# The last four microseconds of a decode kernel: output row in column groups of 228 and 284, the wide part's sums ahead of the direct rows, projection in pieces of 16, 8, 5, 2 and 1 rows

## The chip, the cores and the metric

The kernel runs on one core of one Trainium2 chip. The time is device microseconds of that core, the median of several executions. "Span" is the length of one profiled execution; it is 1.4 to 2.0 us shorter than the time of the same run. Engines: PE does matmuls, DVE and ACT copy and compute, SP issues most of the DMA transfers, POOL hands on semaphores.

## The reference, cut to what matters

```
q = x @ wq                                   # 32 heads of 128
p = softmax(q . k_cache / sqrt(128))         # 16384 keys per head
a = (p . v_cache) @ wo                       # wo: 4096 x 512
b = gated MLP of the same x, @ w_out         # 896 x 512
out = g * a + (1 - g) * b                    # one row of 512, bf16; g = sigmoid(sum(x * gate_w))
```

There is one query row. The two caches are 128 MiB each, and everything else is small beside them. The argument of this document lies entirely in the last product, `@ wo`.

## The kernel before: the parts that matter

The 4096 x 512 matrix `wo` is held as 32 blocks ("rows" below) of 128 partitions x 512 columns. It is loaded in pieces, so that PE can begin before the last byte has come:

```
WO_CUTS = (0, 16, 24, 28, 31, 32)     # pieces of 16, 8, 4, 3 and 1 rows
WIDE = 24                             # rows 0..23 are the "wide part"
NC = 2; DQ = D // NC                  # two column groups of 256
```

The wide part puts four rows side by side into four column groups of the PE array, 512 columns each, so its result `d_ps` is four partial output rows on partitions 0, 32, 64 and 96. ACT copies it to SBUF, and a matmul with a vector of ones then adds up the partitions. The last eight rows (the "direct rows") are added straight into the output row `a_ps`, which is split into two halves on partitions 0 and 32:

```
w_ok = act.op(lambda e: e.copy(out=d_sb[:, :], in_=d_ps), wait=[wide part done])   # line 711
def add(lhsT, rhs, wait, ...):                                                     # line 716
    for s in range(NC):
        matmul(a_ps[32*s : 32*s+1, 0:DQ], lhsT, rhs[:, s*DQ:(s+1)*DQ], accumulate)
for j, (a, b) in pieces:
    for k in range(max(a, WIDE), b):
        add(o2[:, k:k+1], wo[:, k*D:(k+1)*D], wait for piece j)
    if b == 28:
        add(ones_f[:, 0:1], d_sb, [w_ok])            # the wide sums, fp32
# DVE copies half 0 to res, ACT copies half 1 (line 731); SP waits for both,
# then stores the 1024 bytes of res
```
(The fence is shortened: waits and lambdas are written in words, and the loop over the two copies is left out.)

The softmax here doesn't subtract the row's maximum and nothing guards it: scores larger than these inputs give would overflow.

## Time and profile before

The median before the prediction was 652.03 us of three runs; with the runs taken later for comparison it was 651.67 us of six (651.55 to 652.07).

The page of the kernel before, its lines on transfers and on the chain that ended last (the digits are tenths of busy time in 40 slices of the span):

```profile
DMA  9999989999999999999999989999999999999898
...
HBM read 279.58 MB, written 0.00 MB: 430 GB/s over the span
## 4 chain that ended last, share of the span: by engine, by line
DMA 4%; PE 0%; SPq 0%; issue 0%; DVE 0%; ACT 0%; ACTq 0%
```

The kernel is bound by its loads: the DMA engines are busy from end to end. The Trainium skill ("DMA: Bandwidth & Descriptors", Specifications) gives 435 GB/s as the ceiling of the fabric; 430 GB/s over the whole span agrees. (Single slices of 16 us on the page show up to 472 GB/s, so only the whole span is compared.) A change after the last load can move only the tail.

The tail in the timeline of the kernel before (columns: start in us, duration in us, engine, line, operation, output<-input, count; in brackets the idle time just before and what ended it):

```profile
646.45 0.59 ACT L711 COPY d_sb<-ps_all 128x512 f32<-128x512 f32 x1 [6.02 <-PE ps_all L106]
646.92 0.31 PEld L716 LDWEIGHTS ps_all<-bufs,o 128*1 128x1 bf16 x8 [1.02 <-DMA bufs<-in_A_wo_dram]
646.92 0.60 PE L716 MATMUL ps_all<-bufs,o 128*1 128x256 bf16 x8 [0.31 <-DMA bufs<-in_A_wo_dram]
647.25 0.20 PEld L716 LDWEIGHTS ps_all<-d_sb,const-float32-1.0 128*1 128x1 f32 x4
647.36 0.60 PE L716 MATMUL ps_all<-d_sb,const-float32-1.0 128*1 128x256 f32 x4
647.91 0.37 PEld L716 LDWEIGHTS ps_all<-bufs,o 128*1 128x1 bf16 x8 [0.47 <-DMA bufs<-in_A_wo_dram]
647.91 0.60 PE L716 MATMUL ps_all<-bufs,o 128*1 128x256 bf16 x8
648.58 0.36 ACT L731 CAST res<-ps_all 1x256 bf16<-1x256 f32 x1 [1.54 <-PE ps_all L716]
648.58 0.41 DVE L731 CAST res<-ps_all 1x256 bf16<-1x256 f32 x1 [6.09 <-PE ps_all L716]
649.03 0.32 SPq L735 DMA_DIRECT2D out_dram<-res  x1
```

PE does the four rows of the third piece as they land, then the wide sums, which are ready by then, waits for the three rows, and does them and the last row. The pause before 647.91 is a wait for a transfer, not for PE.

### The profile page before, as it was taken

The numbers are of one execution on the slowest core, as the hardware profiler recorded it, in microseconds if no ns is written. First come the engines' busy times: TensorE is split into PE (matmuls) and PEld (weight loads), VectorE is DVE, ScalarE is ACT, GpSimd is POOL, SyncE is SP. The second block draws the span as 40 slices with busy tenths as digits, with TensorE's granted clock in tenths as the row PEclk, the third lists the DMA queues.
The fourth block names the chain that finished last, engine by engine and source line by source line (L and its number), as shares of the span: only waits on it lengthen the run. The fifth ranks groups of instructions, "written<-read, shape, count | busy, mean of one in ns | idle before, by whom it ended". The sixth has DMA issues, their size and how long they took to land. (4 is left out here: it accounts for less than half of the span.)

```text
span 650.2 us, 7735 instructions
## 1 busy us (share of the span) xinstructions
PE 423.0 (65%) x2464; PEld 44.4 (7%) x1304; DVE 336.0 (52%) x159; ACT 45.8 (7%) x112; POOL 2.1 (0%) x10
## 2 busy tenths in 40 slices
PE   0547587847387574747857476584747757478767
PEld 0000000000101000010000101000010100001012
DVE  3457848256380845618265370835629075465600
ACT  2200100000001000010100001000010100001011
POOL 1000000000000000000000000000000000000000
PEclk9959788969779696987969798686978968798999
DMA  9999989999999999999999989999999999999898
GB/s 385 462 419 452 452 387 452 452 439 399 452 452 399 439 452 448 391 452 452 407 431 452 452 387 452 452 423 415 452 452 391 448 452 448 391 431 472 390 432 341
DMA packets 6203, 279.60 MB, mean 430 GB/s; under 512 B 695, under 2 KB 826, under 8 KB 1210
## 3 DMA queue, kind: packets, MB, share of 16 engines
q1 hardware_dynamic: 6194, 279.58, 99.6%
q8 instruction: 1, 0.02, 0.0%
q10 hardware_dynamic: 8, 0.00, 0.0%
HBM read 279.58 MB, written 0.00 MB: 430 GB/s over the span
## 5 line engine op out<-in xcount | busy, mean ns | idle before, releaser
L579 DVE TENSOR_TENSOR bufs<-bufs,qb x64 | 281.5, 4419 | 170.8 <-DVEq L86 170.8
L91 PE MATMUL ps_all<-bufs,ident 128*128 x960 | 261.6, 427 | 0.0
L496 PE MATMUL ps_all<-bufs,ident 128*128 x64 | 28.4, 444 | 153.8 <-PEq L86 153.8
L106 PE MATMUL ps_all<-bufs,p_t 128*8 x1024 | 79.2, 385 | 30.7 <-PEq L86 20.1
L564 DVE TENSOR_REDUCE s_sb<-ps_all 128x64 f32<-128x512 f32 x64 | 44.1, 688 | 95.0 <-DVEq L86 95.0
L91 PE MATMUL ps_all<-zero,ident 128*8 128x512 bf16 (+1 forms) x165 | 58.0, 383 | 0.0
L592 ACT ACTIVATE p_t<-s_sb 64x256 f32 (+1 forms) x32 | 13.3, 414 | 433.4 <-ACTq L86 433.0
L496 PEld LDWEIGHTS ps_all<-bufs,ident 128*128 128x128 bf16 x64 | 6.3, 99 | 367.7 <-issue 367.7
L106 PEld LDWEIGHTS ps_all<-bufs,p_t 128*8 x1024 | 17.9, 82 | 163.7 <-issue 163.5
L531 PE MATMUL ps_all<-pick,d_sb 128*128 128x2 f32 x128 | 16.9, 254 | 16.5 <-PEq L86 16.5
L531 PEld LDWEIGHTS ps_all<-pick,d_sb 128*128 128x128 f32 x128 | 15.7, 192 | 34.7 <-issue 34.7
L601 ACT COPY d_sb<-ps_all 128x512 f32<-128x512 f32 x16 | 9.4, 586 | 104.5 <-ACTq L86 104.5
L606 ACT CAST ps_all<-zero 128x512 f32<-128x512 bf16 x15 | 8.8, 589 | 1.7
L666 DVE RECIPROCAL rl<-ps_all 128x32 f32<-128x32 f32 x1 | 0.4, 357 | 11.3 <-PE ps_all L552 11.3
L669 DVE TENSOR_TENSOR o_sb<-ps_all,rl 128x32 bf16<-128x32 f32 x1 | 0.2, 192 | 11.5 <-PE ps_all L531 11.5
L592 ACT ACTIVATION_READ_ACCUMULATOR p_t<-s_sb (+1 forms) x32 | 5.9, 185 | 0.0
L381 DVE TENSOR_TENSOR bufs<-ps_all,ident 128x896 f32<-128x896 f32 x2 | 2.1, 1086 | 7.3 <-PE ps_all L91 7.3
L321 PE MATMUL ps_all<-xgw,const-float32-1.0 1*128 1x3 f32 x2 | 0.6, 360 | 8.0 <-DVE xgw L317 8.0
L106 PE MATMUL ps_all<-bufs,u 128*1 x14 | 2.6, 372 | 3.3 <-ACT ps_all L427 2.5
L91 PE MATMUL ps_all<-bufs,xb 128*128 x12 | 4.1, 467 | 0.0
L345 PE MATMUL ps_all<-bufs,xb 128*128 x4 | 1.9, 485 | 3.1 <-DMA bufs<-in_B_w_in_dram 3.1
L297 PE MATMUL ps_all<-const-bfloat16-1.0,x_row 1*128 1x128 bf16 x4 | 0.6, 302 | 4.8 <-DMA x_row<-in_A_x_dram 4.8
(76 smaller groups left out, 41.2 us busy)
## 6 DMA issues: line engine op xcount, KB each, us to landing
bufs<-in_A_k_cache_dram SPq DMA_DIRECT2D x2, 4096.0 KB, 35.7
bufs<-in_A_v_cache_dram SPq DMA_DIRECT2D x1, 5120.0 KB, 34.0
bufs<-in_A_wq_dram SPq DMA_DIRECT2D x1, 4096.0 KB, 12.3
bufs<-in_A_v_cache_dram SPq DMA_DIRECT2D x1, 2048.0 KB, 38.6
bufs<-in_A_wo_dram SPq DMA_DIRECT2D x1, 2048.0 KB, 24.6
bufs<-in_B_w_in_dram SPq DMA_DIRECT2D x1, 1792.0 KB, 15.5
bufs<-in_A_v_cache_dram SPq DMA_DIRECT2D x1, 1024.0 KB, 40.6
bufs<-in_A_wo_dram SPq DMA_DIRECT2D x1, 1024.0 KB, 26.7
```

Source lines behind the costliest of these rows:

```text
L91: ins = eng.matmul(out, lhsT=lhsT, rhs=rhs, **flags).ins
L106: ins = eng.matmul(bank[0:m, 0:n], lhsT=lhsT, rhs=rhs, **flags).ins
L297: x_ok = pe.op(lambda e, c=c: e.matmul(m_ps[1][:, c * P:(c + 1) * P], lhsT=x_row[0:1, c::DC], rhs=ones_row[0:1, :], start=True, stop=True) ...
L345: if n else matmul_on(nc, e, lambda: e.matmul(args[0], lhsT=args[1], rhs=args[2], **flags), [at, (xa, 0)]))
L381: dve.op(lambda e, h=h, zh=zh: e.tensor_tensor(out=zm[:, 2 * h * ZB:2 * (h + 1) * ZB].rearrange("p (b m k) -> p b m k", b=2, k=FhC), in0=z ...
L496: matmul_on(nc, e, lambda: e.matmul(s3, lhsT=ident[:, :], rhs=k3[:, :, 0:W], start=True, **flags), [(kw, 0)])
L531: ins = e.matmul(o2, lhsT=d_sb[:, r * Dh:(r + 1) * Dh], rhs=pick[:, r * 2:(r + 1) * 2], start=False, stop=False, skip_group_check=True)
L564: return e.tensor_reduce(out=s_sb[:, c * QK:(c + 1) * QK], in_=s_ps[c % 2].rearrange("p (j w) -> p j w", w=W), axis=AX.X, op=ALU.add)
L579: e.tensor_tensor(out=k3, in0=k3, in1=qi, op=ALU.mult).then_inc(mul_s, 1)
L592: e.activation(out=p_t[rows, bass.ds(at, NG * 8)].rearrange("p (t c) -> p t c", c=8)[:, :, 4 * s:4 * s + 4], in_=s_sb[rows, :].rearrange(" ...
L601: return e.copy(out=d_sb[:, :], in_=d_ps)
L606: e.copy(out=d_ps, in_=zero[:, :]).then_inc(drn_s, 1)
```

## The change

Its intent, as far as the code tells, is to put the wide sums (ready a little after the third piece) ahead of the direct rows, to enlarge the third piece to five rows so that less is left for the end, and to give DVE, whose copy took 0.412 us against ACT's 0.363, the smaller share of the row.

```diff
-NC = 2
-DQ = D // NC
+COLS = (0, 228, 512)
+NC = len(COLS) - 1
-WO_CUTS = (0, 16, 24, 28, 31, 32)
+WO_CUTS = (0, 16, 24, 29, 31, 32)
 ...
-                a_ps[32 * s:32 * s + 1, 0:DQ], lhsT=lhsT, rhs=rhs[:, s * DQ:(s + 1) * DQ],
+                a_ps[32 * s:32 * s + 1, 0:COLS[s + 1] - COLS[s]], lhsT=lhsT,
+                rhs=rhs[:, COLS[s]:COLS[s + 1]],
 ...
+    add(ones_f[:, 0:1], d_sb[:, :], [w_ok])
     for j, (a, b) in enumerate(zip(WO_CUTS[:-1], WO_CUTS[1:])):
         for k in range(max(a, WIDE), b):
             y_ok = add(o2[:, k:k + 1], wo[:, k * D:(k + 1) * D],
                        [(ld_o[j], 16)] if k == a else (), k == H - 1)
-        if b == 28:
-            add(ones_f[:, 0:1], d_sb[:, :], [w_ok])
 ...   # DVE copies columns 0..227, ACT columns 228..511; the mixer uses COLS too
```

More of the change, by code (lines that the diff above doesn't have):

```diff
@@ L441, in pe_mixer @@
             n = len(nc.cur_bb.bb.instructions)
-            for s in range(NC):
+            for s, (a, b) in enumerate(zip(COLS[:-1], COLS[1:])):
                 ins = matmul_on(nc, e, lambda: matmul_at(
-                    nc, e, a_ps, 32 * s, (1, DQ), uk, wk[:, s * DQ:(s + 1) * DQ],
-                    (u[:, 0:1], w_out[:, 0:DQ])),
-                    [(wa, in_setup + 2 * (DC * (HDh + F) + s * DQ)), (ua, 0)])
+                    nc, e, a_ps, 32 * s, (1, b - a), uk, wk[:, a:b],
+                    (u[:, 0:1], w_out[:, 0:b - a])),
+                    [(wa, in_setup + 2 * (DC * (HDh + F) + a)), (ua, 0)])
             registers_first(nc, n)
@@ L725, in gated_mix_kernel @@
                        [(ld_o[j], 16)] if k == a else (), k == H - 1)
-        if b == 28:
-            add(ones_f[:, 0:1], d_sb[:, :], [w_ok])
-    for q in (dve, act):
-        mine = range(NC)[:NC // 2] if q is dve else range(NC)[NC // 2:]
-        for s in mine:
-            ok = q.op(lambda e, s=s, copy=(q is act): (e.copy if copy else e.tensor_copy)(
-                out=res[0:1, s * DQ:(s + 1) * DQ], in_=a_ps[32 * s:32 * s + 1, 0:DQ]),
-                wait=[y_ok] if s in mine[:1] else (), mark=(s == mine[-1]))
+    for s, q in enumerate((dve, act)):
+        ok = q.op(lambda e, s=s, a=COLS[s], b=COLS[s + 1], copy=(q is act):
+                  (e.copy if copy else e.tensor_copy)(
+                      out=res[0:1, a:b], in_=a_ps[32 * s:32 * s + 1, 0:b - a]),
+                  wait=[y_ok], mark=True)
         sp.raw(lambda e, ok=ok: e.wait_ge(*ok))
```

## The prediction

> **What bounds the kernel now.** The transfers. The page gives a mean of 430 GB/s over the span and 98 to 99% busy DMA engines in nearly every slice; the chain that ended last is nearly all one DMA, `bufs<-in_A_wo_dram`, 4.2% of the span. PE is 65% busy, DVE 52%. The Trainium skill ("DMA: Bandwidth & Descriptors", Specifications) puts the fabric ceiling at 435 GB/s; the measured 430 agrees. The change moves no byte less, so only the tail after the last load can change: from 645.6 us to the end at 650.2, under 1% of the span.
>
> **The tail of before, from the timeline and the landings in the trace.** The projection pieces land at 643.13 (16 rows), 645.61 (8), 646.88 (4), 647.87 (3), 648.16 us (1). ACT copies the wide sums at 646.45 for 0.59 us, until 647.04. PE does the 4 rows at 646.92, in pairs of 256-column matmuls that start every 0.108 us (both column groups run side by side), then the fp32 pass over the wide sums at 647.36 (two pairs, 0.214 us each), waits for the 3 rows, starts them at 647.91, and the last row's pair at 648.24 (its weights at 648.20, just after its landing). Copies at 648.58: DVE 0.412 us, ACT 0.363 us. Then the store: 649.03, end 650.2.
>
> **What the change does.**
> 1. Wide sums first: PE now waits for ACT's copy. It starts at about 647.10 instead of 646.92 (a release took 0.04 to 0.07 us elsewhere in this tail): 0.18 us lost in front, but the idle 0.13 us before the 3 rows goes.
> 2. Columns 228 and 284: two column groups stream side by side, so the wider sets the pair's period: 0.108 x 284/256 = 0.119 us, and 0.237 us for an fp32 pair (estimates from the durations above). Over 8 bf16 pairs and 2 fp32 pairs that adds about 0.13 us.
> 3. Pieces of 5, 2, 1 rows: estimated landings 647.2, 647.87, 648.16; total bytes are the same, so the last landing stays.
> 4. Copies: DVE falls by 28 x 1.0 ns (from 0.412 us at 256 columns against 0.19 us at 32), ACT rises by 28 x 0.87 ns (0.587 us at 512 against 0.363 at 256): both near 0.387 us. Saves 0.024 us.
>
> New PE chain: 647.10 + 2 x 0.237 = 647.57; five rows to 648.17; two to 648.40; the last pair starts near 648.41 (landing 648.16 no longer limits). Against 648.24: +0.17; the last matmul 0.01 longer; copies -0.024. Net about **+0.15 us**: PE, not the last landing, would end the tail. The setup's mixer (7 pairs, each 0.011 us longer) is hidden behind loads.
>
> **Predicted time:** 652.2 us, range 651.4 to 653.0 (three runs of before spread over 0.36 us, more than the effect). Faster by over 2%: 0.3%; within 2%: 99.4%; slower by over 2%: 0.3%.
>
> **What the profile would show.** Step 1: the first matmul of the direct sums is fp32, begins just after ACT's copy of the wide sums, and idles on ACT, not DMA. Step 2: pairs 0.118 to 0.120 us apart, with no idle before the 2 rows or the last row. Step 3: the last projection landing as late as before relative to its issue. Step 4: both copies within 0.01 us, near 0.387 us. The chain that ended last should run through PE and ACT's copy.
>
> **What would make it wrong.** If matmuls of the two groups do not go at the wider one's pace, the +0.13 us goes and the result is level. If the last landings come later, PE's extra work hides and only the copies' -0.024 us stays. Drift of some tenths of a us would cover all of this.

## The result, and the profile after

The changed kernel took 651.97 us, the median of six runs (651.71 to 652.43), against 651.67 us for before. The ratio is 1.0004 with a 95% interval of 0.9991 to 1.0017. (Ratios here are the mean time of one kernel's fast runs over that of the other's of the same rounds, so not quite the ratio of the medians quoted.) The run times alone cannot tell whether 0.15 us was added.

The traces can. The chain that ended last, in the kernel after (start in us, duration in us, what):

```profile
...
645.72 0.63 PE ps_all L106 x8
646.35 0.02 issue
646.37 0.59 ACT d_sb L711
646.97 0.04 issue
647.01 1.63 PE ps_all L716 x18
648.64 0.02 issue
648.66 0.39 ACT res L730
```

In the part that the profile can follow back there is no transfer any more. The chain runs through the last matmuls of the wide part, ACT's copy of the wide sums and one unbroken block of PE work. The same chain before consisted almost wholly of the transfer (its last five lines):

```profile
...
619.38 27.50 DMA bufs<-in_A_wo_dram
646.88 0.04 issue
646.92 1.64 PE ps_all L716 x20
648.56 0.02 issue
648.58 0.41 DVE res L731
```

The timeline of the tail after:

```profile
646.37 0.59 ACT L711 COPY d_sb<-ps_all 128x512 f32<-128x512 f32 x1 [6.01 <-PE ps_all L106]
647.01 0.09 PEld L716 LDWEIGHTS ps_all<-d_sb,const-float32-1.0 128*1 128x1 f32 x4 [1.19 <-ACT d_sb L711]
647.01 0.65 PE L716 MATMUL ps_all<-d_sb,const-float32-1.0 128*1 128x228 f32 x4 [0.47 <-ACT d_sb L711]
647.20 1.10 PEld L716 LDWEIGHTS ps_all<-bufs,o 128*1 128x1 bf16 x16
647.39 1.23 PE L716 MATMUL ps_all<-bufs,o 128*1 128x228 bf16 x16
648.66 0.39 ACT L730 CAST res<-ps_all 1x284 bf16<-1x284 f32 x1 [1.70 <-PE ps_all L716]
648.66 0.38 DVE L730 CAST res<-ps_all 1x228 bf16<-1x228 f32 x1 [6.24 <-PE ps_all L716]
649.14 0.32 SPq L734 DMA_DIRECT2D out_dram<-res  x1
```

The first idle time is now ended by `ACT d_sb`, and no later PE line has an idle time. In the trace's finer records only the narrow group's last matmul still waits for the last row: it starts at 1.769 us after the start of ACT's copy, 0.044 us after the landing at 1.725. It costs nothing, as the wide group is busy until well after. ACT's copy of the wide sums started at times from 646.37 to 647.56 us in the fourteen profiles, because the loads before it vary from run to run. That is why differences of 0.1 us drown in the run times, and why all tails below are measured from the start of that copy (times in us; the starts and the landings are the trace's own records, finer than the printed lines). "Last landing" is the arrival of the last row of `wo`.

| kernel | last landing | last matmul starts | result copies start | store starts | span ends |
|---|---|---|---|---|---|
| before | 1.70 | 1.79 | 2.131 | 2.583 | 3.74 |
| after | 1.73 | 1.97 | 2.288 | 2.765 | 3.92 |

So the tail became 0.18 us longer: the last matmul starts 0.176 us later, the result copies 0.157, and the store 0.182. Counted from the landing of the eight rows, which lies 0.84 us before the start of the copy in both, the store starts at 3.42 and 3.60 us: the same 0.18.

### The profile page after: what moved, and what is told of

Read it like the earlier page. It is cut to its first block, busy times and chain, and to the rows that moved or that the text cites. A ratio compares the mean times of both kernels' runs of the same rounds, so it can differ in the third digit from the quotient of the medians.

```text
span 650.3 us, 7735 instructions
## 1 busy us (share of the span) xinstructions
PE 422.3 (65%) x2464; PEld 45.0 (7%) x1304; DVE 335.9 (52%) x159; ACT 45.8 (7%) x112; POOL 2.2 (0%) x10
## 5 line engine op out<-in xcount | busy, mean ns | idle before, releaser
L106 PE MATMUL ps_all<-bufs,xb 128*64 x32 | 3.6, 380 | 0.0
```

Source lines behind the costliest of these rows:

```text
L106: ins = eng.matmul(bank[0:m, 0:n], lhsT=lhsT, rhs=rhs, **flags).ins
```

## The experiments

The theory is this. (1) After ACT's copy PE has no gap, so its work sets the end. (2) The two column groups stream side by side, and the wider one sets the pace of a pair. (3) The order and the cuts are worth little by themselves. Rivals: the wait for ACT's copy alone costs the 0.18 us; the later landing of the five-row piece costs it; or something outside the tail does. The change has three parts, so all eight combinations were run, six of them new (the columns of the mixer go with those of the output row). Each kernel gave the correct result. Each tail is that of one profile. For the first four runs below (after_again, columns, order and cuts undone) the trace kept is another execution than the one shown and measured here; its starts after ACT's copy agree to 0.01 us wherever no landing decides them. "T" is the time from the start of ACT's copy of the wide sums to the end of the later result copy.

### The changed kernel again

No edit.

> The changed kernel unchanged, to separate its time from drift. Measure T: from the start of ACT's copy of the wide sums to the end of the later result copy (before 2.54 us, after 2.67 us in their profiles). My theory (the tail is all there is, and PE's chain sets it): T 2.67 again, and a median of 0.1 to 0.2 us over before's in the same rounds. Rival (something outside the tail costs the 0.3 us between the two medians): a gap of 0.3 us or more again, with T unchanged.

Its median was 651.86 us of five runs, against 652.09 us for before in the same rounds: ratio 0.9998 (0.9984 to 1.0011). T was 2.675 us in both profiles of this kernel, and every start in the tail that no landing decides agrees to about 0.001 us. A gap of 0.3 us between the medians did not come back. The interval would still allow one, but in the traces nothing outside the tail is later: the eight rows land at 645.61 us in before, and at 645.53 and 645.60 in after and in the kept trace of this run. The expected 0.1 to 0.2 us is not visible in the run times either.

### Columns undone

```diff
-COLS = (0, 228, 512)
+COLS = (0, 256, 512)
```

> Sums first and pieces 16, 8, 5, 2, 1, but columns 256 and 256. My theory (the pair of column groups goes at the pace of its wider part): pairs 0.108 us apart, fp32 pairs 0.214, T 2.57 us, of which the copies take 0.41. Rival (the loss is the wait for ACT's copy at the front, the width does not matter): T stays near 2.67 to 2.70.

T was 2.590 us. The timeline of this kernel:

```profile
647.50 0.60 PE L716 MATMUL ps_all<-d_sb,const-float32-1.0 128*1 128x256 f32 x4 [0.47 <-ACT d_sb L711]
647.71 0.98 PEld L716 LDWEIGHTS ps_all<-bufs,o 128*1 128x1 bf16 x16
647.93 1.04 PE L716 MATMUL ps_all<-bufs,o 128*1 128x256 bf16 x16
```

The wait for ACT is the same 0.47 us, and the 16 direct matmuls take 1.04 us in place of 1.23. Pairs start 0.109 us apart here, and the wide matmuls 0.1207 us apart in the kernel after; the fp32 pairs are 0.215 against 0.239. The store starts at 2.627, only 0.044 us later than before. So of the 0.182 us the columns account for 0.138, given the other two parts: 0.112 up to the start of the result copies, which is PE's pace, and the rest behind it, in the copies and the wait for them (see "One semaphore for both copies"). The rival "the wait costs it, the width does not matter" falls. Median 652.05 us, ratio 1.0000 (0.9986 to 1.0014).

### Order undone

```diff
-    add(ones_f[:, 0:1], d_sb[:, :], [w_ok])
     for j, (a, b) in enumerate(...):
         for k in range(max(a, WIDE), b): ...
+        if j == 2:
+            add(ones_f[:, 0:1], d_sb[:, :], [w_ok])
```

> Columns 228 and 284 and pieces 16, 8, 5, 2, 1, but the wide sums after the five rows, as before. My theory: the five rows can start only when they land, 0.78 us after ACT's copy starts, and nothing fills the time until then, so T is longer still: 2.82 us. Rival (sums first is what costs): T falls to before's 2.54.

T was 2.824 us. The first direct matmul waits for its piece, and the sums come after:

```profile
647.32 0.77 PE L716 MATMUL ps_all<-bufs,o 128*1 128x228 bf16 x10 [0.63 <-DMA bufs<-in_A_wo_dram]
647.71 0.30 PEld L716 LDWEIGHTS ps_all<-d_sb,const-float32-1.0 128*1 128x1 f32 x4
647.81 0.76 PE L716 MATMUL ps_all<-d_sb,const-float32-1.0 128*1 128x228 f32 x4
```

The store starts at 2.912, so in the company of the other two parts, sums first saves 0.147 us. The order is not the culprit. Median 652.16 us, ratio 1.0004 (0.9988 to 1.0019).

### Cuts undone

```diff
-WO_CUTS = (0, 16, 24, 29, 31, 32)
+WO_CUTS = (0, 16, 24, 28, 31, 32)
```

> Columns 228 and 284 and sums first, but pieces 16, 8, 4, 3, 1. My theory: the PE chain started by ACT's copy runs without a gap, no landing limits it, so the cuts do nothing: T 2.67 us, same starts as after. Rival (the later landing of the bigger third piece costs): T under 2.6.

T was 2.673 us and the store started at 2.762: the same tail as after, to 0.003 us. Behind an unbroken PE chain the cuts do nothing, and the rival of the later landing falls.

The kept trace of this kernel shows one thing more. In it PE ran at half clock from 643.56 to 646.97 us, so the wide part ended late: ACT's copy started 1.31 us after the landing of the eight rows, in place of 0.84 in after. The store still started 2.764 us after ACT's copy, so the whole delay of 0.47 us reached the store. Median 652.37 us, ratio 1.0008 (0.9992 to 1.0023).

### Columns alone

Before, with columns 228 and 284 only.

> Only the columns 228 and 284, the rest as before. My theory: PE waits for the 3 rows anyway, so the wider part costs only 4 pairs' 0.012 us and the last row starts at 1.82 us after ACT's copy instead of 1.79; the copies take 0.387 instead of 0.41: T 2.53 us, level with before's 2.54. Rival (the wide part costs 0.13 us wherever it stands): T 2.65.

The profile fell in an interval of half clock, so T (2.192 us) can't be compared with the number expected: what the columns cost alone stays unmeasured, and the rival of 2.65 untested. In it ACT's copy started 1.25 us after the eight-row piece landed, against 0.84 in the profile of before. The wide part ran slowly:

```profile
643.20:646.60 3.40, 3.33 (x26) 0.60 (x24) 0.00 (x0) 0.00 (x0) 0.00 (x0) 0.51 1.00 408
```

This is the view of busy time by windows; after the window and its length come the busy time and count of PE, PE's weight loads, DVE, ACT and POOL, then the granted PE clock, the busy share of the DMA engines and GB/s. The clock is 0.51 here. In the same window of before and after it is 1.00. The Trainium skill ("TensorE: Matmul & The Clock Gate", Part 1) describes a half-rate state that is decided in windows of 3.4 us which do not start with the kernel; the trace's clock record agrees, with a half-clock interval of 3.4 us from 643.1 us.

What the run still shows is how well the order of before hides such a delay: the copy was 0.41 us late, but the store started only 0.11 us later than in before, both counted from the landing of the eight rows (1.25 + 2.282 against 0.84 + 2.583). Median 651.67 us, ratio 0.9997 (0.9982 to 1.0013).

### Order alone

Before, with the wide sums first only.

> Only the wide sums first, columns 256 and pieces 16, 8, 4, 3, 1. My theory: the chain starts 0.64 us after ACT's copy starts, two fp32 pairs of 0.214, eight pairs of 0.108: last pair at 1.82, T 2.57 us (+0.03). Rival (the order costs all of the 0.13): T 2.67.

T was 2.642 us, but in this run the last row landed 0.13 us later than usual (1.84 us after ACT's copy started, against 1.67 to 1.76 in the other ten profiles without a late wide part), and the last pair waited for it, as the profile says:

```profile
648.28 0.08 PEld L716 LDWEIGHTS ps_all<-bufs,o 128*1 128x1 bf16 x2 [0.18 <-DMA bufs<-in_A_wo_dram]
```

The seventh pair started at 1.722 us, where it also started with columns undone (1.723). Without the late landing T would have been about 2.59 us by that comparison, which is an estimate. The rival of 2.67 is not shown wrong by this run alone; the run with columns undone, which has the same order, does that. Median 651.90 us, ratio 0.9999 (0.9984 to 1.0014).

### Cuts alone

Before, with pieces 16, 8, 5, 2, 1 only; the sums come after the five rows.

> Only the pieces 16, 8, 5, 2, 1, columns 256, the sums after the five rows. My theory: five rows from 0.78 to 1.32, fp32 until 1.75, three pairs, T 2.72 us (+0.18): this cut needs the sums in front of it. Rival (the cuts are free as the last landing does not move): T 2.54.

T was 2.743 us and the store started at 2.781, 0.198 us later than before, with the last landing where it was (1.74 against 1.70). Five rows that start only at 0.79 us push the sums back, and the sums push back the rest. The cut needs the sums in front of it, as expected; so point (3) of the theory above holds for the cuts only with the sums there. Median 651.85 us, ratio 1.0002 (0.9987 to 1.0017).

### A second width: 128 and 384

```diff
-COLS = (0, 228, 512)
+COLS = (0, 128, 512)
```

> As after, but columns 128 and 384: the pace law at a second size. My theory: pairs 0.162 us apart, fp32 pairs 0.32, ACT's copy 0.474, T 3.26 us (+0.6 on after). Rival (the two groups share one stream of 512 columns, 0.108 us a pair whatever the split, and the 0.12 us after has another cause): pairs 0.108 apart, T about 2.65.

T was 3.257 us. The wide matmuls started 0.162 us apart, and the fp32 ones 0.32. The pace goes with the wider group at 256, 284 and 384 columns: 0.109, 0.121 and 0.162 us (the mean of seven steps each). The Trainium skill ("TensorE: Matmul & The Clock Gate", Back-to-back issue gap) gives N/2.4 + 2.5 ns as the gap of isolated matmuls of N columns at full clock, and says that it over-counts at large N where each matmul has its own weight load. The formula makes 109, 121 and 163 ns. The runs agree with it for the wider of two streams side by side, although every matmul here has its own weight load. The narrow group runs ahead and gains nothing: here four of its bf16 matmuls start before the first bf16 matmul of the wide group (at 1.289 us), though the program puts the two groups of each row in turn. Its median was 652.96 us, ratio 1.0014 (0.9999 to 1.0029).

This profile too had the half clock in the wide part (0.53), so ACT's copy started 1.16 us after the landing of the eight rows in place of 0.84. Here, with sums first, the starts after ACT's copy were those expected at full clock, so the 0.32 us went straight through to the store, as the 0.47 us did in the kept trace of "cuts undone". The two schedules differ in this: before has a pause that absorbs most of a late wide part, after has none.

### A version meant to win: four column groups

```diff
-COLS = (0, 228, 512)
+COLS = (0, 128, 256, 384, 512)         # order and pieces as before
+    # DVE copies partitions 0..63, ACT 64..127, 128 elements each, to res[128, 128]
-    sp.op(lambda e: e.dma_start(out=out.rearrange("a b d -> (a b) d"), in_=res[:, :]),
+    sp.op(lambda e: e.dma_start(out=out.rearrange("a b (s c) -> (a b s) c", s=NC),
+                                in_=res[0:32 * NC:32, :]),
```

> A version meant to beat both: four column groups of 128 columns on partitions 0, 32, 64, 96, order and pieces as before, DVE copies partitions 0 to 63 and ACT 64 to 127 (128 elements per partition), the store takes four rows of 256 bytes. My theory (groups side by side go at the pace of the widest, copies cost by elements per partition): a row every 0.054 us, the last landing (1.72 us after ACT's copy of the wide sums starts) limits again, last row at 1.76, result copies 0.29 us, T 2.34 us, 0.2 us under before, if the store takes no longer than before (1.14 us from its issue to the end of the span). Rival: four short rows in the store or the wider copy give it back, and the span is level.

The gain came and was given back. A row took 0.055 us, the copies 0.261 and 0.284. This profile also had the half clock in the wide part, so it is compared from the last landing: the store started 0.70 us after it, against 0.88 in before. But the store then took 1.66 us until the end of the span, against 1.16. The span ends 2.36 us after the last landing, against 2.04. The store in four_groups and in before, by the view of one source line (minimum, median and maximum of SP's time for the issue in ns):

```profile
L734 SPq DMA_DIRECT2D out_dram<-res x1: 625/625/625, 648.9 to 648.9; - x1
```

```profile
L735 SPq DMA_DIRECT2D out_dram<-res x1: 318/318/318, 649.0 to 649.0; - x1
```

Median 651.99 us against 651.70, ratio 1.0004 (0.9990 to 1.0018).

### The store in two rows

Before, with `res` on partitions 0 and 32 and the store in two rows of 512 bytes.

> Before, with the result kept on partitions 0 and 32, and the store of two rows of 512 bytes. The store of one row of 1024 bytes took 1.16 us from its start to the end of the span in ten profiles, that of four rows of 256 bytes 1.66 us. If rows under 512 bytes are what costs: 1.16 us here. If more than one row (more DMA engines, more to report) costs: 1.3 to 1.7 us.

It took 1.61 us to the end of the span, and 609 ns to issue:

```profile
L735 SPq DMA_DIRECT2D out_dram<-res x1: 609/609/609, 650.1 to 650.1; - x1
```

The Trainium skill ("DMA: Bandwidth & Descriptors", Specifications) names 512 bytes as the least transfer that reaches full rate. That is not what costs here, since two rows of 512 bytes cost nearly as much as four of 256. More than one row does: from the start of the issue to the first packet it took 1.21 us against 0.75, and of these 0.46 us the issue itself accounts for 0.29. The two rows also lie on two partitions in place of one, which was not separated. Why is open. Median 652.01 us, ratio 1.0001 (0.9986 to 1.0017).

### One semaphore for both copies

```diff
-                  wait=[y_ok], mark=True)
-        sp.raw(lambda e, ok=ok: e.wait_ge(*ok))
+                  wait=[y_ok], inc=(res_s, 1))
 ...
+          wait=[(res_s, 2)], inc=(st_out, 16))     # the store waits for this alone
```

> The changed kernel, but both result copies count up one semaphore and the store waits for it alone. In the traces the store of before starts 0.452 us after the copies start (copies 0.363 and 0.412), that of after 0.477 (both about 0.385). My theory: SP waits for two semaphores in turn, ACT's first, and the store cannot start until 0.09 us after ACT's copy ends or 0.04 after DVE's, so balancing the copies gained nothing; with one semaphore the store starts 0.43 us after the copies start, 0.05 us sooner than in after. Rival (the store needs 0.09 us after any last copy, or the copies of equal length disturb each other): 0.477 again.

This was made because of a small surprise: after shortened the longer copy from 0.412 to 0.387 us, yet the store started later after the copies' start (0.477 against 0.452). In both kernels the trace shows that SP waits for ACT's semaphore in one instruction, and the store carries the wait for DVE's. In after, where ACT ends last, the store starts 0.09 us after it; in before, where DVE ends last, 0.04 us. With one semaphore the store started 0.414 us after the copies, 0.063 us sooner than in after. The rest of the tail is that of after:

```profile
648.85 0.39 ACT L730 CAST res<-ps_all 1x284 bf16<-1x284 f32 x1 [1.70 <-PE ps_all L716]
648.85 0.38 DVE L730 CAST res<-ps_all 1x228 bf16<-1x228 f32 x1 [6.25 <-PE ps_all L716]
649.26 0.32 SPq L733 DMA_DIRECT2D out_dram<-res  x1
```

The Trainium skill ("Perfetto Trace Analysis", Identifying Dependency Chains) says that an instruction that waits on several engines may have further waits put in front of it as separate instructions; the trace agrees (the source of this kernel itself writes two waits, and one of them stays an instruction of its own), and the wait that comes first in the queue is the one to end early. So with two semaphores the equal shares that the change made for the copies were worse for the store than 256 and 256 with ACT ahead; no other split was run. Median 652.04 us, ratio 1.0005 (0.9991 to 1.0018).

### A second version meant to win: sums in bf16, one semaphore

```diff
 # on "order undone" with the one semaphore of above
-    w_ok = act.op(lambda e: e.copy(out=d_sb[:, :], in_=d_ps), ...)
+    w_ok = act.op(lambda e: e.copy(out=w_sb[:, :], in_=d_ps), ...)     # w_sb is bf16
-            add(ones_f[:, 0:1], d_sb[:, :], [w_ok])
+            add(ones_b[:, 0:1], w_sb[:, :], [w_ok])
```

> A version meant to beat both: columns 228 and 284, pieces 16, 8, 5, 2, 1, sums after the five rows, the wide sums in bf16 (one pass in place of two), the two copies on one semaphore. My theory: the sums cost 0.12 us in place of 0.48, PE is free again when the 2 rows land, the last landing limits: the store starts 2.52 us after ACT's copy of the wide sums starts (before 2.58, after 2.77), if PE's clock is at full speed in the wide part; from the landing of the 8 rows 3.36 us (before 3.42, after 3.60). In the run times it is within noise. Rival (two fp32 passes are not what fills PE): 2.7 or more.

The store started at 2.549 us (before 2.583, after 2.765) and the span ended at 3.70 (3.74 and 3.92), though the last row landed at 1.76 in this run:

```profile
648.91 0.66 PE L718 MATMUL ps_all<-bufs,o 128*1 128x228 bf16 x6
649.28 0.08 PEld L718 LDWEIGHTS ps_all<-bufs,o 128*1 128x1 bf16 x2 [0.19 <-DMA bufs<-in_A_wo_dram]
```

PE waits for the last row again, so the last landing limits and not PE, as the theory asks. One bf16 pass costs one pair's time (0.121 us between the wide matmuls around it) in place of two fp32 pairs of 0.239. The gain on before is 0.04 us of tail, and it lies behind PE: the result copies start no sooner (2.135 against 2.131, with a last landing 0.06 us later), but the store follows them by 0.414 us in place of 0.452, through the balanced copies and the one semaphore. What bf16 does shows against "order undone", which differs up to the result copies in nothing else: they start 0.30 us sooner. The median was 651.53 us of five runs against 651.89 us for before, ratio 0.9994 (0.9980 to 1.0007): the interval holds 1, so the run times do not show a gain, and the traces show one of the size just given. The price is that the wide sums are rounded to bf16 before they are added.

All tails together, in us from the start of ACT's copy of the wide sums. Rows with a star had the half clock in the wide part, so their landings come early against that start.

| kernel | last landing | last matmul starts | result copies start | store starts | span ends |
|---|---|---|---|---|---|
| before | 1.70 | 1.79 | 2.131 | 2.583 | 3.74 |
| order alone | 1.84 | 1.89 | 2.228 | 2.680 | 3.83 |
| cuts alone | 1.74 | 1.99 | 2.327 | 2.781 | 3.94 |
| columns alone * | 1.33 | 1.48 | 1.805 | 2.282 | 3.44 |
| order and cuts (columns undone) | 1.71 | 1.84 | 2.176 | 2.627 | 3.78 |
| columns and cuts (order undone) | 1.73 | 2.12 | 2.437 | 2.912 | 4.07 |
| columns and order (cuts undone) | 1.73 | 1.97 | 2.287 | 2.762 | 3.92 |
| after, first and second profile | 1.73, 1.67 | 1.97, 1.97 | 2.288, 2.288 | 2.765, 2.764 | 3.92, 3.92 |
| 128 and 384 * | 1.41 | 2.43 | 2.788 | 3.347 | 4.50 |
| four groups * | 1.29 | 1.35 | 1.641 | 1.992 | 3.65 |
| store in two rows | 1.70 | 1.76 | 2.095 | 2.547 | 4.16 |
| one semaphore | 1.70 | 1.97 | 2.288 | 2.702 | 3.86 |
| bf16 sums | 1.76 | 1.81 | 2.135 | 2.549 | 3.70 |

## Why the prediction was right, and where it was not

- **The bound and the time.** Right. The kernel is bound by loads that the change does not touch; 652.2 us was predicted and 651.97 us measured, inside the range. That is no test of the mechanism: the range is 1.6 us wide, ten times the effect, and holds a change of nothing as well. The run times do not resolve the predicted +0.15 us: the median moved by +0.30 us in the first comparison and by -0.23 us in the second, both within the spread.
- **Step 1, sums first.** Right. The first direct matmul is fp32 and idles on ACT. It began 0.639 us after ACT's copy started; the prediction had 0.65. The net of 0.18 us lost in front and 0.13 us of pause saved was measured by undoing the columns: 0.044 us.
- **Step 2, the wider group sets the pace.** Right. 0.1207 us a pair (0.119 predicted), 0.239 for fp32 (0.237), and 0.128 us on the start of the last matmul (0.13) between after and columns undone.
- **Step 3, the cuts.** Right that the last landing stays (1.73 against 1.70) and that the chain of PE no longer waits for it. The prediction did not say what the runs showed besides: the cuts do nothing behind the unbroken chain, and cost 0.198 us alone.
- **Step 4, the copies.** The durations were right (0.384 and 0.387 us), but "Saves 0.024 us" failed. The store started 0.025 us later after the copies' start, not sooner, since SP waits for the two engines one after the other and ACT, the first in its queue, now ended last. That makes +0.025 us in place of -0.024. The run with one semaphore shows it.
- **The sum.** The +0.15 was put together from +0.17 for the start of the last matmul, +0.01 for its length and -0.024 for the copies. Measured were +0.176, -0.019 and +0.025, together +0.182. The middle term failed too: the result copies started 0.321 us after the start of the last matmul, in place of 0.340 in before. It is 0.34 in all five profiles with two groups of 256, where the last two matmuls start together, and 0.32 in the six with 228 and 284 where the narrow group's last matmul started at least 0.1 us earlier; the cause was not tested. So two misses of opposite sign partly cancel, and that the sum is off by only 0.03 us is in part luck.
- **The chain.** Right: it runs through PE and ACT's copy.

What stays open: whether the half clock, which made the wide part late in 3 of the 14 profiles of the table and in one more that was kept, also hit unprofiled runs of the two kernels, and so whether after is slower on average by more than the 0.18 us of its undisturbed tail. Both profiles of after were at full clock there.

## What to carry to other kernels

When a tail waits for its last transfer, look for the pause in the compute engine before you rearrange: work moved into the pause is free, and work that fills it entirely makes that engine the new limit and takes away the slack against a late start. Split a row unevenly over parallel column groups only if the matmuls have time to spare, as each pair goes at the pace of the wider part. And balance two engines' copies by when the waiting engine can go on, not by their durations: with waits in a queue, the first waited for should end first, or both should count up one semaphore.

## What the Trainium skill lacked or had wrong

- "TensorE: Matmul & The Clock Gate" (Part 3) and "TensorEngine Tiling (Array Packing)" give no time for groups of unequal size side by side. Neither says that unequal ones go at the pace of the widest: 0.109, 0.121 and 0.162 us a pair at 256, 284 and 384 columns in the wider group, with 512 columns in all each time.
- "Perfetto Trace Analysis" (Identifying Dependency Chains) mentions the extra waiting instruction but no cost. Here the engine waited for first released the store 0.09 us after it ended, the other 0.04 us, and a single semaphore made the store start 0.063 us sooner.
- "DMA: Bandwidth & Descriptors" gives a least size for full rate (512 bytes) but no cost of a second row in a tiny store. One row of 1024 bytes took 0.32 us to issue and 1.16 us to the end of the span; two rows of 512 took 0.61 and 1.61; four of 256 took 0.62 and 1.66.
- The half-rate windows of "TensorE: Matmul & The Clock Gate" (Part 1) were seen as described, so nothing is wrong there: 3.4 us at half clock, at a place that differs from run to run. In 3 of the 14 profiles of the table, and in the kept trace of "cuts undone", one covered the wide part to its end or nearly so and made it finish 0.32 to 0.47 us later.
